# A range guard that tests a bound instead of the last outputs, and a load of its flag that moves ahead of the last eviction

## The chip, the cores and the metric

The kernel runs on one core of one Trainium2 chip. The metric is device time in microseconds for one launch, lower is better. A core has five engines that run in parallel, each through its own queue in order: TensorE (PE; its weight loads are listed as PEld), VectorE (DVE), ScalarE (ACT), GpSimd (POOL) and SyncE (SP, which here issues DMA transfers). Queue entries of an engine's sequencer (loads of registers, branches, semaphores, DMA issues) stand in the profile with a "q" behind the engine's name. PE writes into PSUM, which is divided into banks; DVE and ACT read the banks out ("evict" them) into SBUF, and a bank can take a new matmul only after that.

## The reference

Attention over keys that are pooled 4x4 from an image, with one weight matrix for both keys and values, followed by a gated feed-forward block. Four images, 12288 queries each, 768 pooled keys, 128 channels, 1536 hidden features.

```python
kv_pool = kv.reshape(B, H // r, r, W // r, r, C).mean(axis=(2, 4))
k = v = kv_pool.reshape(B, -1, C) @ w_sr
s = (q @ k.transpose(0, 2, 1)) / np.sqrt(C)
a = np.exp(s - s.max(-1, keepdims=True))
a /= a.sum(-1, keepdims=True) + 1e-09
x = (a @ v).reshape(B * S, D)
out = (np.maximum(x @ w_gate, 0.0) * (x @ w_val)) @ w_out
```

The kernel leaves out the subtraction of the row's maximum and carries x without the division by the row sum: since the block is homogeneous of degree two in x (for positive factors), the output is multiplied at the end by the square of the inverse row sum (`square`, `scale`). That holds only while nothing leaves the range of the 16-bit types, so the kernel ends with a guard: a flag is computed, and if it says that something was out of range, a slow general version (`general`) recomputes everything.

## The kernel before, in words

The 49152 queries are worked in 96 tiles of 512 (`NT` = 96, `k` is the tile's number). Every tile goes through five steps: scores (word `s`, PE) and their exponentials (`e`, ACT, with row sums by accumulation); a DMA transpose of the exponentials on SP (`a_turn`); x, the values weighted by them (`x`, six PE matmuls), evicted to 16 bits by `keep_values` (word `kA`); 12 hidden blocks, each a value matmul `v`, its eviction on ACT `y` (line 142), a gate matmul `g`, and the gated product on DVE `h` (line 526); and 12 output matmuls `o` with the eviction of the output.

The order on every engine is written out by hand, as lists of words. In one pass of the main loop (slot `k`) the words work on different tiles: scores of tile k, x of tile k-2, hidden blocks of tile k-3 (`kF`), output of tile k-4 (`kO`). `STEADY` is the list while there are scores (k < 96), `DRAIN` the list of slots 96 and 97, `LAST` that of slot 98, in which there are only the outputs of tile 94 and the hidden blocks of tile 95, in the order `o v y g h` for block 0, 1, 2 and so on. `out_last` then makes the output of tile 95. The parts of `DRAIN` that matter here are:

```python
... v5 v3 h6 g8 y5 g3 v2 o0 kA y3 o1 v11 g5 y2 h8 y11 o2 v7 ...
... g9 v10 y10 o8 v4 h9 g1 o9 o10 y4 g4 h1 o11 g10 h4 h10 oT
```

Matmul results other than the scores go to six PSUM banks. `bank()` hands out the one that has been in the list of free banks longest, and `freed()` puts a bank at the end of that list where its eviction is written, so the word lists fix which matmul waits for which eviction. The scores have two wide buffers of their own (`wides`).

At the end of a slot, word `oT` evicts the output. For tiles up to 92 that is `out_turn`: a 32x32 block transpose on DVE (line 556), the scaling on POOL (line 561), an addition of the outputs' first columns into `seen` (line 562) and DMA stores, which are handed out one at a time behind the `o` words of the next slot on POOL's and SP's queues (line 946). For tile 93 `out_scale` evicts and scales on DVE (line 593) at the end of slot 97, for tile 94 on ACT (line 591) after `LAST`. `out_store` issues the store and adds a column to `seen` on POOL (line 605). Tile 95 is evicted in three parts by `out_last`: two on DVE, the last on ACT.

The guard before has three sources. `sums_checked` (ACT, lines 832 and 835, in slot 97) tests that the row sums lie between two bounds. `seen_checked` (DVE, lines 838 and 839) turns that, and `seen` (which is infinite or not a number if an output of tiles 0 to 94 was) into 16-bit marks. `last_checked` (line 844) does so for the last part's output, counts the marks with a PE matmul (line 848) and reduces them on DVE to one integer (line 849). `values_load` (line 988) loads it into a register of every engine, and `tc.If` branches on it.

The pooled keys of images 1 to 3 are made during the image before (`image_step`), one pair of key blocks every four slots: loads, sums on POOL, in slot 6 after the pair's beginning a block transpose and a write to DRAM on SP (`turn_blocks`, line 360), then four reads of that block into `kvT` (line 825), which wait in SP's queue for that write, in slot 8 the projection on PE (word `P`) and its eviction on DVE (word `pk`, line 346), and in slots 9 and 11 DMA transposes.

Of the kernel before, what the change touches and what calls it, by code (L numbers as in the profile page):

```python
# [9 lines left out]
FP32 = mybir.dt.float32  # L10
FP16 = mybir.dt.float16
AF = mybir.ActivationFunctionType
ALU = mybir.AluOpType
# [3 lines left out]
def kernel(  # L17
# [23 lines left out]
    nc = tc.nc  # L41

    B, N, C = q.shape
# [15 lines left out]
    LEAD = GRP  # L59
    AT_BUFS = 4  # L60
    qk_scale = 1.0 / math.sqrt(C)
    SUM_MOST, SUM_LEAST = 32.0 * J, J / 8.0

    assert C == 128 and N % T == 0 and J == 128 * NJC and D_FF == 128 * NFB
    assert NFB == 2 * NJC and NST % GRP == 0 and W // r == 8 and HC == 64
# [66 lines left out]
    def freed(ps):  # L132
        free_banks.append(bank_numbers.pop(id(ps))[0])
        return ps
# [310 lines left out]
    def keep_values(k):  # L445
        xT = work.tile([128, NS, 128], FP16, tag="xT", bufs=4, name="xT")
        xTs[k] = xT.rearrange("c s p -> c (s p)")
        nc.vector.tensor_copy(xTs[k], freed(x_banks.pop(k)))  # L448

    x_count = {}  # L450

# [85 lines left out]
    def out_proj(k, fb):  # L537
        if k >= NT - 3:
            if fb == 0:
                o_banks[k] = bank([128, NS, 128])  # L540
            for s in range(NS):
                out_add(k, fb, s, o_banks[k][:, s, :], fb == 0 and s == 0)
            return
        first = k not in o_banks
        if first:
            o_banks[k], o_left[k] = bank([128, T]), NFB
        o_left[k] -= 1
        nc.tensor.matmul(  # L548
            o_banks[k], wo16[:, fb, :], hTs[k][:, fb, :], start=first, stop=o_left[k] == 0
        )  # L550
# [47 lines left out]
    def out_store(k, own, queue=nc.sync):  # L598
        queue.dma_start(
            out[k // GRP * GRP * T : (k // GRP + 1) * GRP * T, :].rearrange(  # L600
                "(p i s) c -> i p s c", p=128, i=GRP
            )[k % GRP][:, own], o_sbs[k][:, own],
        )
        if own.stop == NS and k < NT - 1:
            nc.gpsimd.tensor_tensor(
                seen[:, 0:NS], seen[:, 0:NS], o_sbs[k][:, :, 0], op=ALU.add
            )
        if own.stop == NS:
            for tiles in (hTs, o_banks, o_sbs):
                del tiles[k]  # L610

    def out_last(k):
        parts = [bank([128, 2, 128]), bank([128, 1, 128]), bank([128, 1, 128])]
        owns = [slice(0, 2), slice(2, 3), slice(3, 4)]
        o_banks[k] = None

        def add(s, fb0, fb1):
            n = max(s - 1, 0)
            for fb in range(fb0, fb1):
# [12 lines left out]
        keep(0, nc.vector)  # L632
        add(2, held, NFB)
        keep(1, nc.vector)
        seen_checked()
        add(3, 0, NFB)
        o_sb = o_sbs[k]
        keep(2, nc.scalar, nc.scalar)
        last_checked(o_sb)

    ctx.enter_context(tc.manual_schedule())

# [2 lines left out]
    make_identity(nc, ident)  # L645
    ident16 = const.tile([128, 128], FP16)
    nc.gpsimd.tensor_copy(ident16, ident)
    out_of_range = const.tile([1, 1], mybir.dt.int32)
    ones = const.tile([128, 32], FP16)
    nc.gpsimd.memset(ones, 1.0)  # L650
    lead_scale = const.tile([128, LEAD, NS * 4], FP32)
# [2 lines left out]
    nc.gpsimd.memset(too_much, -SUM_MOST)  # L654
    seen = const.tile([128, NS * 4], FP32)
    nc.gpsimd.memset(seen, 0.0)
    bad = const.tile([128, 2], FP32)
    bad16 = const.tile([128, 22], FP16)
    enough = const.tile([128, 1], FP32)
    nc.gpsimd.memset(enough, SUM_LEAST)  # L660
    nc.gpsimd.memset(kv16[:, :, :, 2 * C : 2 * C + 16], 1.0 / X_SCALE)
# [155 lines left out]
    def image_step(b, at, step):  # L817
        for pair in range(NJC // 2):
            since = at - 4 * pair
            if since in (0, 1) and step in (2, 8):  # L820
                kv_load(b, pair, [2 * since + step // 8])
            elif since in (3, 4) and step == 3:
                pool_pixels(nc.gpsimd, b, pair, since - 3)
            elif since == 6 and moves and step > 4:
                nc.sync.dma_start(*moves.pop())
            elif since in (9, 11) and step == 1:
                turn_values_dma(b, 2 * pair + since // 11)

    def sums_checked():
        past = work.tile([128, NT * NS], FP32, tag="kv_s3", bufs=2, name="past")  # L830
        sums = row_sums.rearrange("t k s -> t (k s)")
        nc.scalar.activation(
            past, sums, AF.Relu, scale=1.0, bias=too_much, accum_out=bad[:, 0:1]
        )
        nc.scalar.activation(past, sums, AF.Relu, scale=-1.0, bias=enough, accum_out=bad[:, 1:2])

    def seen_checked():
        nc.vector.tensor_scalar(bad16[:, 0:2], bad, 0.0, None, op0=ALU.is_gt)
        nc.vector.tensor_scalar(
            bad16[:, 2:18], seen, 0.0, 0.0, op0=ALU.mult, op1=ALU.not_equal  # L840
        )

    def last_checked(o_sb):
        nc.vector.tensor_scalar(
            bad16[:, 18:22], o_sb[:, :, 0], 0.0, 0.0, op0=ALU.mult, op1=ALU.not_equal
        )
        count = wides[0].tile([128, 1024], FP32, tag="wide", name="count_ps")
        nc.tensor.matmul(count[0:1, 0:22], ones[:, 0:1], bad16, start=True, stop=True)
        nc.vector.tensor_reduce(
            out_of_range, count[0:1, 0:22], axis=mybir.AxisListType.X, op=ALU.max  # L850
        )

    def general():
# [74 lines left out]
    for k in range(LEAD + 2, last + 1):  # L928
        g, ph = divmod(k, GRP)
        if ph % 2:  # L930
            q_turn_two(g + 1, ph - 1)
        if ph:
            q_load(g + 2, [[0], [2], [3]][ph - 1])
        b = k // NST + 1
        at = k % NST - 4
        kO, kF, kV = k - LAG - 1, k - LAG, k - 2
        words = STEADY if k < NT else DRAIN if k < last else LAST
        for word in words:
            head, n = word.rstrip("0123456789"), int(word.lstrip("abcdefghijklmnopqrstuvwxyzADPT") or 0)
            if head == "o":  # L940
                out_proj(kO, n)
                if ph == 1 and n == NFB // 2:
                    q_load(g + 2, [1])
                for queue in (nc.gpsimd, nc.sync):
                    if out_moves and n >= 2:
                        queue.dma_start(*out_moves.pop())  # L946
                if spread:
                    spread_scales(*spread.pop(0))
                if b < B:
                    image_step(b, at, n)  # L950
            elif head == "oT":
                if k == last - 1:
                    sums_checked()
                if kO < NT - 3:
                    out_moves.extend(out_turn(kO))
                elif k < last:
                    out_scale(kO, nc.vector, slice(0, NS))
                    out_store(kO, slice(0, NS))
            elif head in ("v", "y", "g", "h"):
                if kF < NT:  # L960
                    {"v": value_proj, "y": keep_value, "g": gate_proj, "h": gated}[head](kF, n)
            elif head in ("s", "e"):
                if k < NT:
                    {"s": score_block, "e": exp_block}[head](k, n)
                    if head == "e" and n % 2:
                        a_turn(k, n - 1, n + 1)
            elif head == "r":
                if LEAD < k <= NT and k % 2 == 0:
                    invert(k - 2)
                    spread += [(k - 2, j) for j in range(4)]  # L970
            elif head in ("tb", "P", "pk"):
                pair, since = divmod(at - 6 if head == "tb" else at - 8, 4)
                if b < B and 0 <= pair < NJC // 2 and since == 0:
                    if head == "tb":
                        moves.extend(turn_blocks(b, pair))
                    elif head == "P":
                        project(b, pair)
                    else:
                        keep_projected(b, pair)
            elif LEAD <= kV < NT:  # L980
                if head == "x":
                    values(kV, n)
                else:
                    keep_values(kV)
    out_scale(last - LAG - 1, nc.scalar, slice(0, NS))
    out_store(last - LAG - 1, slice(0, NS))
    out_last(last - LAG)
    flag = nc.values_load(
        out_of_range[0:1, 0:1],
        skip_runtime_bounds_check_because="it is a count of partitions that is only compared with 0",  # L990
    )
    with tc.If(flag > 0, preferred_fallthrough_block=False):
        general()


# [28 lines left out]
```

## Time and profile before

| what | value |
|---|---|
| time, median of 3 runs | 1026.57 us (1026.33 to 1027.56) |
| time of the profiled execution | 1027.61 us |
| its span on the core | 1025.7 us |
| PE busy | 1017.4 us, 99% |
| ACT busy | 919.4 us, 90% |
| DVE busy | 867.9 us, 85% |
| POOL busy | 545.0 us, 53% |
| granted TensorE clock | 0.998 |
| last 5.7 us (from 1020.0): PE busy in the first 4 us of it | 1.15 us |

The span is what the profile shows between the first and the last recorded instruction; the time of the same execution is 1.9 us longer. Times in the views are us from the span's start. A line of the timeline has start, length, engine, line of the kernel, operation, output and inputs, shape, the number of instructions merged in it and, in brackets, how long the engine was idle before and who ended that. A line of the groups has the busy time of all its instructions, the mean length of one in ns, and the idle time just before them. The chain of waits follows the end of the span back to what released each step; PE makes up 98% of it.

### The profile page before, as it was taken

The numbers are of one execution on the slowest core, as the hardware profiler recorded it, in microseconds if no ns is written. First come the engines' busy times: TensorE is split into PE (matmuls) and PEld (weight loads), VectorE is DVE, ScalarE is ACT, GpSimd is POOL, SyncE is SP. The second block draws the span as 40 slices with busy tenths as digits, with TensorE's granted clock in tenths as the row PEclk, the third lists the DMA queues.
The fourth block names the chain that finished last, engine by engine and source line by source line (L and its number), as shares of the span: only waits on it lengthen the run. The fifth ranks groups of instructions, "written<-read, shape, count | busy, mean of one in ns | idle before, by whom it ended". The sixth has DMA issues, their size and how long they took to land.

```text
span 1025.7 us, 17625 instructions
## 1 busy us (share of the span) xinstructions
PE 1017.4 (99%) x5029; PEld 487.4 (48%) x5029; DVE 867.9 (85%) x1451; ACT 919.4 (90%) x1930; POOL 545.0 (53%) x1410
## 2 busy tenths in 40 slices
PE   8999999999999999999999999999999999999998
PEld 5444444444444444444444444444444444444445
DVE  4888888888888888888888888888888888888897
ACT  4999898989999999999999999989999999999986
POOL 3388857344447576545434856754434543443342
PEclk9999999999999999999999999999999999999999
DMA  9999999987898999788879899977776978776641
GB/s 315 160 176 180 167 207 163 147 127 125 139 194 157 187 180 172 137 127 139 125 132 202 175 176 197 150 134 134 127 132 113 144 118 129 124 128 114 108 83 43
DMA packets 475750, 153.53 MB, mean 150 GB/s; under 512 B 451585, under 2 KB 465921, under 8 KB 475649
## 3 DMA queue, kind: packets, MB, share of 16 engines
q1 hardware_dynamic: 453184, 126.08, 67.6%
q0 software_dynamic: 22032, 25.19, 17.0%
q10 hardware_dynamic: 432, 1.11, 0.3%
q8 instruction: 40, 0.66, 0.3%
q14 instruction: 62, 0.50, 0.2%
HBM read 53.94 MB, written 26.35 MB: 78 GB/s over the span
## 4 chain that ended last, share of the span: by engine, by line
PE 98%; DMA 1%; DVE 0%; issue 0%; SPq 0%; ACT 0%; POOL 0%; DVEq 0%; POOLq 0%
PE bank_ps L507 24%; PE bank_ps L518 24%; PE bank_ps L548 23%; PE wide_ps L398 12%; PE bank_ps L440 12%; DMA kv_in<-in_kv_dram 1%; PE bank_ps L532 1%; PE bank_ps L379 1%; PE bank_ps L457 1%; PE wide_ps L337 0%; PE bank_ps L301 0%; PE bank_ps L315 0%; PE bank_ps L210 0%; PE bank_ps L475 0%; DVE kv_s L273 0%
## 5 line engine op out<-in xcount | busy, mean ns | idle before, releaser
L526 DVE SCALAR_TENSOR_TENSOR hT<-bank_ps,val 128x512 f16<-128x512 f32 x1152 | 728.1, 680 | 104.5 <-PE bank_ps L518 83.9
L142 ACT CAST val<-bank_ps 128x512 f16<-128x512 f32 x1149 | 628.4, 596 | 43.5 <-PE bank_ps L507 23.1
L507 PE MATMUL bank_ps<-xT,wv 128*128 128x512 f16 x1152 | 420.6, 379 | 0.0
L518 PE MATMUL bank_ps<-xT,wg 128*128 128x512 f16 x1152 | 376.0, 379 | 0.0
L548 PE MATMUL bank_ps<-hT,wo 128*128 128x512 f16 x1116 | 348.5, 379 | 0.0
L403 ACT ACTIVATE a<-wide_ps 128x768 f16<-128x768 f32 x368 | 302.1, 821 | 44.1 <-PE wide_ps L398 44.1
L398 PE MATMUL wide_ps<-kv,qT 128*128 128x512 f16 x736 | 179.7, 326 | 0.0
L440 PE MATMUL bank_ps<-aT,kv 128*128 128x512 f16 x552 | 178.8, 379 | 0.0
L548 PEld LDWEIGHTS <-wo 128*128 128x128 f16 x1116 | 109.2, 98 | 132.2 <-issue 1.1
L518 PEld LDWEIGHTS <-wg 128*128 128x128 f16 x1152 | 112.7, 98 | 122.6 <-issue 0.6
L561 POOL TENSOR_TENSOR o_sb<-o_t,scale 128x512 f32<-128x512 f32 x89 | 93.2, 1047 | 140.2 <-issue 122.4
L507 PEld LDWEIGHTS <-wv 128*128 128x128 f16 x1152 | 112.6, 98 | 105.3 <-issue 0.6
L424 POOL COPY scale<-square 32x8 f32<-32x8 f32 x736 | 141.3, 192 | 28.6
L417 POOL TENSOR_TENSOR square<-inverse 128x8 f32<-128x8 f32 x46 | 9.3, 202 | 240.0 <-DVE inverse L415 233.5
L946 POOL DMA_DIRECT2D out_dram<-o_sb x208 | 130.3, 632 | 1.9 <-DMA q<-in_q_dram 1.6
L398 PEld LDWEIGHTS <-qT 128*128 128x128 f16 x736 | 72.0, 98 | 86.9 <-issue 0.2
L448 DVE CAST xT<-bank_ps 128x512 f16<-128x512 f32 x92 | 63.6, 691 | 31.6 <-PE bank_ps L440 31.6
L440 PEld LDWEIGHTS <-kv 128*128 128x128 f16 x552 | 54.0, 98 | 65.1
L403 ACT ACTIVATION_READ_ACCUMULATOR a<-wide_ps 128x1 f32 x368 | 76.1, 207 | 0.0
L556 DVE STREAM_TRANSPOSE o_t<-bank_ps 128x512 f32<-128x512 f32 x93 | 65.4, 703 | 0.2 <-PE bank_ps L507 0.2
L163 POOL DMA_DIRECT2D q<-in_q_dram x84 | 48.8, 581 | 7.1 <-issue 7.1
L257 POOL TENSOR_TENSOR s<-kv_in 128x512 f32<-128x512 f32 x36 | 45.1, 1282 | 0.7
(97 smaller groups left out, 232.9 us busy)
## 6 DMA issues: line engine op xcount, KB each, us to landing
kv_in<-in_kv_dram SPq DMA_DIRECT2D x42, 512.0 KB, 5.3
out_dram<-o_sb SPq DMA_DIRECT2D x177, 64.0 KB, 3.5
q<-in_q_dram POOLq DMA_DIRECT2D x88, 128.0 KB, 4.5
out_dram<-o_sb POOLq DMA_DIRECT2D x176, 64.0 KB, 4.1
aT<-a SPq DMA_TRANSPOSE x184, 5.0
kv_line<-in_kv_dram SPq DMA_DIRECT2D x4, 512.0 KB, 9.9
placed<-blocks SPq DMA_DIRECT2D x9, 128.0 KB, 2.4
kvT<-placed SPq DMA_DIRECT2D x36, 32.0 KB, 1.9
```

The costliest lines, as they stand in the source:

```text
L142: nc.scalar.copy(to, what)
L398: nc.tensor.matmul(s_ps[:, j0 * 128 : j1 * 128], qT, kv16[:, b, j0:j1, 0:C], start=True, stop=True)
L403: nc.scalar.activation(a16s[k][:, s, :], s_banks.pop(s)[:, 0:J], AF.Exp, scale=qk_scale, accum_out=a_sums[k // 2][:, k % 2, s : s + 1],)
L424: nc.gpsimd.tensor_copy(to[32 * b : 32 * (b + 1), :, :, j], squares[k // 2][32 * j : 32 * (j + 1)])
L440: nc.tensor.matmul(x_banks[k], kv16[:, k // NST, jc, C : 2 * C], aT[:, jc], start=first, stop=x_left[k] == 0,)
L507: nc.tensor.matmul(proj_banks["v", k, fb], wv16[:, fb * 128 : (fb + 1) * 128], xTs[k], start=True, stop=True,)
L518: nc.tensor.matmul(proj_banks["g", k, fb], wg16[:, fb * 128 : (fb + 1) * 128], xTs[k], start=True, stop=True,)
L526: nc.vector.scalar_tensor_tensor(hTs[k][:, fb, :], freed(proj_banks.pop(("g", k, fb))), 0.0, vals.pop((k, fb)), op0=ALU.max, op1=ALU.mult,)
L548: nc.tensor.matmul(o_banks[k], wo16[:, fb, :], hTs[k][:, fb, :], start=first, stop=o_left[k] == 0)
L556: nc.vector.transpose(o_t, freed(o_banks.pop(k)))
L561: nc.gpsimd.tensor_tensor(to, o_by, scale.to_broadcast([128, NS, 4, 32]), op=ALU.mult)
L946: queue.dma_start(*out_moves.pop())
```

## The change

- `keep_values` evicts x of tiles 94 and 95 on ACT instead of DVE.
- The outputs of tiles 94 and 95 are no longer looked at (`seen` ends with tile 93). Instead the guard bounds the gated products of these two tiles: per channel the largest |x| of them (`most_of`, one DVE reduction of 128x512 for each tile, at word `oT` of slots 96 and 97; a DVE maximum of the two), times, per block of 256 hidden features, the largest weight of that channel (`widest_of`, twelve DVE reductions of 128x256 over the 16-bit gate and value weights, at word `pk` of slots 74 to 85), summed over the channels by a matmul. The product of the largest sum for the gate and the largest for the value must be at most 60000.
- The test of `seen` (times zero, on POOL) and the row sums' marks go through another matmul. Both matmuls (fp32) stand in PE's queue behind `o6` of `LAST`, and four one-partition DVE steps behind `h5` make one integer, which is now 1 for "in range".
- The flag is loaded inside `out_last`, after the last matmul and ahead of the last eviction on ACT. The branch stays at the end.
- The four reads into `kvT` are issued in slot 7 (from `o2` on) instead of slot 6 (from `o5` on).

```diff
+    SUM_MOST, SUM_LEAST, GATED_MOST = 32.0 * J, J / 8.0, 60000.0
...
     def keep_values(k):
...
-        nc.vector.tensor_copy(xTs[k], freed(x_banks.pop(k)))
+        if k < NT - 2:
+            nc.vector.tensor_copy(xTs[k], freed(x_banks.pop(k)))
+        else:
+            nc.scalar.copy(xTs[k], freed(x_banks.pop(k)))
...
-        if own.stop == NS and k < NT - 1:
+        if own.stop == NS and k < NT - 2:
             nc.gpsimd.tensor_tensor(
                 seen[:, 0:NS], seen[:, 0:NS], o_sbs[k][:, :, 0], op=ALU.add
...
         keep(1, nc.vector)
-        seen_checked()
         add(3, 0, NFB)
-        o_sb = o_sbs[k]
+        flag = nc.values_load(
+            in_range[0:1, 0:1],
...
+        )
         keep(2, nc.scalar, nc.scalar)
-        last_checked(o_sb)
+        return flag
...
+    bad = const.tile([128, 18], FP32)
+    ones32 = const.tile([128, 1], FP32)
+    nc.gpsimd.memset(ones32, 1.0)
...
-            elif since == 6 and moves and step > 4:
+            elif since == 7 and moves and step > 1:
                 nc.sync.dma_start(*moves.pop())
...
+    def widest_of(n):
+        nc.vector.tensor_reduce(
+            widest[:, n : n + 1], (wg16, wv16)[n // NJC][:, n % NJC * 256 : (n % NJC + 1) * 256],
+            axis=mybir.AxisListType.X, op=ALU.max, apply_absolute_value=True,
+        )
+
+    def most_of(k):
+        if NT - 2 <= k < NT:
+            nc.vector.tensor_reduce(
+                most[:, k - NT + 2 : k - NT + 3], xTs[k],
+                axis=mybir.AxisListType.X, op=ALU.max, apply_absolute_value=True,
+            )
+
     def seen_checked():
-        nc.vector.tensor_scalar(bad16[:, 0:2], bad, 0.0, None, op0=ALU.is_gt)
...
+        nc.vector.tensor_tensor(most[:, 0:1], most[:, 0:1], most[:, 1:2], op=ALU.max)
+        nc.gpsimd.tensor_scalar(bad[:, 2:18], seen, 0.0, None, op0=ALU.mult)
+
+    def checked():
+        count = wides[0].tile([128, 1024], FP32, tag="wide", name="count_ps")
+        nc.tensor.matmul(count[0:1, 0:18], ones32, bad, start=True, stop=True)
+        nc.tensor.matmul(
+            count[0:1, 512 : 512 + 2 * NJC], most[:, 0:1], widest, start=True, stop=True
+        )
+        reach = const.tile([1, 2], FP32)
+        nc.vector.tensor_reduce(
+            reach, count[0:1, 512 : 512 + 2 * NJC].rearrange("o (w n) -> o w n", w=2),
+            axis=mybir.AxisListType.X, op=ALU.max,
+        )
+        nc.vector.tensor_reduce(
+            found[:, 0:1], count[0:1, 0:18], axis=mybir.AxisListType.X, op=ALU.add
+        )
         nc.vector.tensor_scalar(
...
+            found[:, 1:2], reach[:, 0:1], reach[:, 1:2], GATED_MOST, op0=ALU.mult, op1=ALU.is_le
+        )
+        nc.vector.scalar_tensor_tensor(
+            in_range, found[:, 0:1], 0.0, found[:, 1:2], op0=ALU.is_le, op1=ALU.mult
         )
...
                 out_proj(kO, n)
+                if k == last and n == 2:
+                    seen_checked()
+                if k == last and n == 6:
+                    checked()
...
                     sums_checked()
+                if NT <= k < last:
+                    most_of(k - 2)
...
                 pair, since = divmod(at - 6 if head == "tb" else at - 8, 4)
+                if head == "pk" and k < NT and 0 <= k - (B - 1) * NST - 2 < 2 * NJC:
+                    widest_of(k - (B - 1) * NST - 2)
...
-    out_last(last - LAG)
-    flag = nc.values_load(
...
-    with tc.If(flag > 0, preferred_fallthrough_block=False):
+    flag = out_last(last - LAG)
+    with tc.If(flag < 1, preferred_fallthrough_block=False):
         general()
```

More of the change, by code (lines that the diff above doesn't have):

```diff
@@ L61 @@
     qk_scale = 1.0 / math.sqrt(C)
-    SUM_MOST, SUM_LEAST = 32.0 * J, J / 8.0
+    SUM_MOST, SUM_LEAST, GATED_MOST = 32.0 * J, J / 8.0, 60000.0
     assert C == 128 and N % T == 0 and J == 128 * NJC and D_FF == 128 * NFB
@@ L634, in out_last @@
         keep(1, nc.vector)
-        seen_checked()
         add(3, 0, NFB)
-        o_sb = o_sbs[k]
+        flag = nc.values_load(
+            in_range[0:1, 0:1],
+            skip_runtime_bounds_check_because="it is 0 or 1 and only compared with 0",
+        )
         keep(2, nc.scalar, nc.scalar)
-        last_checked(o_sb)
+        return flag
     ctx.enter_context(tc.manual_schedule())
@@ L647 @@
     nc.gpsimd.tensor_copy(ident16, ident)
-    out_of_range = const.tile([1, 1], mybir.dt.int32)
+    in_range = const.tile([1, 1], mybir.dt.int32)
     ones = const.tile([128, 32], FP16)
@@ L656 @@
     nc.gpsimd.memset(seen, 0.0)
-    bad = const.tile([128, 2], FP32)
-    bad16 = const.tile([128, 22], FP16)
+    bad = const.tile([128, 18], FP32)
+    ones32 = const.tile([128, 1], FP32)
+    nc.gpsimd.memset(ones32, 1.0)
+    widest = const.tile([128, 2 * NJC], FP32)
+    most = const.tile([128, 2], FP32)
+    found = const.tile([1, 2], FP32)
     enough = const.tile([128, 1], FP32)
@@ L835, in sums_checked @@
         nc.scalar.activation(past, sums, AF.Relu, scale=-1.0, bias=enough, accum_out=bad[:, 1:2])
-    def seen_checked():
-        nc.vector.tensor_scalar(bad16[:, 0:2], bad, 0.0, None, op0=ALU.is_gt)
+    def widest_of(n):
[9 more added lines that the diff above has]
+            )
+    def seen_checked():
+        nc.vector.tensor_tensor(most[:, 0:1], most[:, 0:1], most[:, 1:2], op=ALU.max)
[14 more added lines that the diff above has]
+        )
         nc.vector.tensor_scalar(
-            bad16[:, 2:18], seen, 0.0, 0.0, op0=ALU.mult, op1=ALU.not_equal
+            found[:, 1:2], reach[:, 0:1], reach[:, 1:2], GATED_MOST, op0=ALU.mult, op1=ALU.is_le
         )
[L843 to L850, printed above, removed]
+        nc.vector.scalar_tensor_tensor(
+            in_range, found[:, 0:1], 0.0, found[:, 1:2], op0=ALU.is_le, op1=ALU.mult
         )
@@ L986 @@
     out_store(last - LAG - 1, slice(0, NS))
-    out_last(last - LAG)
[L988 to L991, printed above, removed]
-    with tc.If(flag > 0, preferred_fallthrough_block=False):
+    flag = out_last(last - LAG)
+    with tc.If(flag < 1, preferred_fallthrough_block=False):
         general()
```

## The prediction

> **What bounds the kernel now.** First the page's busy table and its costliest groups.
>
> ```profile
> PE 1017.4 (99%) x5029; PEld 487.4 (48%) x5029; DVE 867.9 (85%) x1451; ACT 919.4 (90%) x1930; POOL 545.0 (53%) x1410
> ...
> L507 PE MATMUL bank_ps<-xT,wv 128*128 128x512 f16 x1152 | 420.6, 379 | 0.0
> ```
>
> TensorE (PE) has work from end to end: its 1152 value matmuls have 0.0 us idle ahead of them. Two kinds of change move the end: what makes PE late, and what follows its last matmul (a stretch that I call the tail). So next the timeline of the last 5 us, the lines of the flag's load and of the program's end.
>
> ```profile
> 1020.29 0.62 DVE L593 TENSOR_TENSOR o_sb<-bank_ps,square 128x256 f32<-128x256 f32 x2 [0.90 <-PE bank_ps L532]
> ...
> 1021.07 0.37 ACT L591 ACTIVATE o_sb<-bank_ps,square 128x128 f32<-128x128 f32 x1 [1.31 <-POOL seen L605]
> 1021.17 0.38 SPq L599 DMA_DIRECT2D out_dram<-o_sb  x1
> 1021.47 0.36 ACTq L599 DMA_DIRECT2D out_dram<-o_sb  x1
> 1021.47 0.17 DVE L844 TENSOR_SCALAR bad<-o_sb 128x4 f16<-128x4 f32 x1 [0.40 <-ACT o_sb L591]
> 1021.69 0.17 PE L848 MATMUL count_ps<-bad,ones 128*1 128x22 f16 x1 [0.71 <-DVE bad L844]
> 1021.90 0.17 DVE L849 TENSOR_REDUCE out_of_range<-count_ps 1x1 int32<-1x22 f32 x1 [0.26 <-PE count_ps L848]
> ...
> L988 SPq TENSOR_LOAD <-out_of_range x1: 482/482/482, 1022.1 to 1022.1; - x1
> ...
> L1019 SPq EVENT_SEMAPHORE  x12: 27/28/28, 1023.5 to 1024.2; - x12
> L1019 SPq DRAIN  x2: 7/10/13, 1024.3 to 1024.3; - x2
> ...
> L1019 POOLq DRAIN  x1: 1692/1692/1692, 1023.2 to 1023.2; - x1
> ```
>
> The last matmul ends at 1020.98. After it comes a chain: the eviction, three guard steps, the flag's load on every engine at 1022.1, a branch, and the end. GpSimd's (POOL's) drain of 1.69 us starts at 1023.2 and ends at 1024.9; SyncE (SP) is through with its semaphores at 1024.35 and waits 0.6 us for that. 0.8 us of closing semaphores bring the span to 1025.74. The last store (1021.47) lands by 1023.2, the row's 1.7 us.
>
> Last the places where VectorE (DVE) and ScalarE (ACT) feed PE after the last attention tile.
>
> ```profile
> 994.13 1.07 ACT L142 CAST val<-bank_ps 128x512 f16<-128x512 f32 x2 [0.90 <-PE bank_ps L507]
> ...
> 995.44 0.38 PE L518 MATMUL bank_ps<-xT,wg 128*128 128x512 f16 x1
> ...
> 1009.82 1.29 DVE L526 SCALAR_TENSOR_TENSOR hT<-bank_ps,val 128x512 f16<-128x512 f32 x2
> 1011.03 0.68 DVE L593 TENSOR_TENSOR o_sb<-bank_ps,square 128x512 f32<-128x512 f32 x1
> 1011.62 1.28 DVE L526 SCALAR_TENSOR_TENSOR hT<-bank_ps,val 128x512 f16<-128x512 f32 x2
> ...
> 1011.76 0.10 PEld L507 LDWEIGHTS <-wv 128*128 128x128 f16 x1 [0.17 <-DVE o_sb L593]
> ```
>
> A 512-wide DVE step starts 0.60 us after the one before (1011.03, 1011.62), a cast on ACT 0.48 us after (1.07 for two less 0.59 for one). At 1011.76 PE stands waiting for DVE's L593: there DVE's lateness is PE's at once.
>
> **The change, part by part.**
>
> Tail. Flag and guard leave it. POOL can load the flag, branch and drain (1.69 us) while PE still works on the last tile. What is left is SP: its last store is issued at 1021.17 for 0.38 us, then it loads the flag at 1021.60 instead of 1022.10, and its whole walk moves by 0.50 us: done at 1023.86, with the store landed by 1023.2. The closing 0.8 us then start 1.06 us earlier than now (1024.95 less 1023.86, less 0.03 for the signal). Term: -1.06. ACT's load goes ahead of the last eviction: 0.49 us between 1019.76, where the eviction before ends, and 1021.07; hidden, and without the cover it would be up to 0.5. Bounds: -1.1, and 0 if POOL's drain is tied to the others' end.
>
> The x casts of tiles 94 and 95 move from DVE (L448) to ACT, in word kA of DRAIN, behind y5 and ahead of y3. They put y3 and what follows 0.48 us back. The six banks go out in the order in which they came free; walking DRAIN's words, g5 takes the bank that y3 frees. y3 (the second cast of 994.13) ends at 995.20, g5 starts at 995.44: a reserve of some 0.2. PE is 0.28 late, and 0.05 more at v7, behind y2. Term +0.33. In the second drain tile (g5 at 1004.52, y3 over at 1004.27) the same gives +0.32. Bounds: 0 (the cast slips into one of ACT's gaps, 0.87 to 0.90 us just ahead of y5) and +0.48 each.
>
> DVE gets 0.60 back per cast, and gives it for `most_of`, a reduction of 128x512, at oT. In tile 96 it delays L556's transpose by 0.6, but the next user of that bank has a reserve of 0.4 and DVE catches up where its cast was: in the +0.32. In tile 97 it stands between h10 (1010.43) and L593 (1011.03), where PE waits already, and the relief came 7 us too early (DVE follows its inputs after 1005, so it was not ahead). Term +0.60. No row shows such a reduction; bounds: 0.2, the start-to-start of L849 on 22 elements, and 1.2, two casts; I take the cast, which has as many elements. The Trainium skill, "VectorE: DVE Perf Modes", section "The perf-mode tier table", says that a reduction has no faster mode for 16-bit data, only one element a cycle, which speaks against placing it here. By it the price is the cast's, with a mode of two elements a cycle it would be near 0.33 and the sum 0.27 less; no row here shows which.
>
> Guard in the last tile. Two fp32 matmuls in PE's queue after o6, at most 0.1 us each by L301's 0.11 us steps; their inputs are ready (DVE's maximum behind h1, POOL's product after L605 at 1012.06, ACT's sums since 1010.9). DVE then gets four one-partition steps between h5 and h6: two free ones at 0.07 us (L838 to L839), two that need the result before them at some 0.2 (0.17 and a signal), 0.54 in all. DVE's reserve per step is 0.05 (12 steps in 7.77 us against 0.60 each), and PE's v9 takes the bank of h6 (over at 1016.12) at 1016.36: 0.19. So 0.54 - 0.05 - 0.19 = +0.30 on PE, the matmuls' 0.2 inside it, for what waits on PE isn't late twice. Bounds +0.1 and +0.7. The 30 matmuls of `out_last` before h10 leave 0.4 us for DVE to be level again.
>
> `widest_of`: twelve reductions 128x256, one in each of tiles 74 to 85, at word pk. L346, a DVE step of that width at that word, took 0.34 us start to start (168.76 to 169.11), and PE stood still after one of nine. But those tiles hold an extra projection, which gives DVE time that here is missing; the walk leaves about 0.30 of reserve at pk, so 0.00 to 0.05 each. Term +0.3 (0 to +0.6).
>
> Image. Four kvT reads in nine places leave the tile in which SP waits for the block's write.
>
> ```profile
> SPq L825 <- DMA placed<-blocks: 20.3, 9, 3.7
> ```
>
> That frees 2.3 us of SP each time, past two transposes of a and one of q, whose users come a tile or more later. PE shows no wait on any of it, and the projection still has a tile's length after the reads. Term 0 (-0.5, the few stalls in the middle of the trace, to +0.2). A memset on POOL in the opening, 0.1 us, is hidden: POOL waits there for DVE until about 10 us.
>
> Sum: -1.06 + 0.33 + 0.32 + 0.60 + 0.30 + 0.3 = +0.8 us. The span of 1025.7 becomes 1026.5. The profiled run took 1027.61, which is 1.04 over the median of the three runs; +0.8 on that median is 1027.4. The terms on PE are lateness that small gaps may take up, so I go a little lower: 1027.2.
>
> **Rivals.**
>
> All is hidden but the tail: the banks' reserves hold the added work. 1026.57 - 1.06 = 1025.5. For it: ACT's gaps, DVE's 15% of idle time. Against: those gaps stand elsewhere, and PE already waits for L593.
>
> Nothing comes off the tail: POOL's 1.69 us drain ends when the other engines do, wherever it starts. 1026.57 + 1.85 = 1028.4. For it: no other engine's drain is over 0.09 us. Against: nothing that POOL started is open then.
>
> Slower: reductions cost more than a cast of the same size. It is `widest_of` that decides: above the 0.30 of reserve each 0.1 us makes PE 1.2 us later over twelve tiles. With 0.45 us for 256 elements the sum is 0.8 + 12 x 0.105 = +2.06, and from there on the kernel is slower than a measurement's noise. At two cycles an element (0.6 and 1.1 us) it is 0.8 + 3.2 + 0.9 = +4.9, or 1031.5. For it: no row of a long reduction. Against: cast, gate product and transpose all take one element a ns.
>
> The flag says out of range, and everything is computed again: milliseconds. The bound (a sum over channels of the largest |x| by the widest weight) lies far under 60000 for weights and inputs of this size.
>
> **How the numbers follow.** Forecast 0.70 (1026.5 to 1028.3 by the bounds), all hidden 0.14, nothing off the tail 0.08, dear reductions 0.06, the rest 0.02. The range takes in the rival below and most of the one above: 1025.6 to 1028.6. 0.2% is 2.05 us, about what a measurement of this kernel can tell from no change. All but the dear reductions and the far ends of the others stay inside: same 0.86, slower 0.10, faster 0.04 (a gain from the image's move that I can't see).
>
> **What would show it.** Right: POOL's drain over before PE's last matmul, SP's twelve semaphores ending the span, PE idle ahead of L518 near 995.5 and 1004.8 for about 0.3 us each, 0.6 us more ahead of the third value matmul of the last tile, 0.3 us after the counts; each 128x512 reduction near 0.60 us. Wrong: PE's last matmul at its old distance from the start, a drain of POOL still at the end, or the twelve tiles with `widest_of` more than 0.06 us longer than the tiles after them.

## Result, and the profile after

| what | before | after |
|---|---|---|
| time, median of 11 runs each, alternating | 1026.40 us (1026.22 to 1027.56) | 1029.06 us (1028.19 to 1030.34) |
| time of the profiled execution | 1027.61 us | 1029.25 us |
| its span | 1025.7 us | 1027.5 us |

The ratio is 1.0025, 95% interval 1.0016 to 1.0035: the change makes the kernel 2.7 us slower. The prediction was 1027.2 (1025.6 to 1028.6), so it gave too low a time.

Two measures are used from here on, both read from the trace. The **PE part** is the time from the first value matmul of the 61st hidden tile, in the steady middle of the run, to the end of PE's last output matmul: 372.39 us before, 374.33 after, **+1.94**. The **tail** is the time from that end to the end of the span: 4.76 us before, 5.58 after, **+0.82**. Together +2.76, which is the difference of the medians (+2.66). The spans differ by 1.8 only, since the profiled execution of before lost about 1.0 us more in its opening than most others.

The PE part first. Busy table and groups of the page of after:

```profile
PE 1017.8 (99%) x5032; PEld 486.7 (47%) x5032; DVE 870.5 (85%) x1464; ACT 921.3 (90%) x1932; POOL 545.1 (53%) x1411
...
L510 PE MATMUL bank_ps<-xT,wv 128*128 128x512 f16 x1152 | 420.8, 379 | 0.7 <-DVE o_sb L596 0.6
```

PE's work is the same but for three count matmuls in the records. What was 0.0 us of idle time before the value matmuls is 0.7, and 0.6 of it is one wait for an eviction on DVE (L596, the L593 of before). The timeline of after shows that wait, what stands ahead of it on DVE, and the other places where PE is late (start, length, engine, line):

```profile
994.60 0.38 PE L510 MATMUL bank_ps<-xT,wv 128*128 128x512 f16 x1
995.09 0.38 PE L521 MATMUL bank_ps<-xT,wg 128*128 128x512 f16 x1
...
1001.58 0.68 DVE L854 TENSOR_REDUCE most<-xT 128x1 f32<-128x512 f16 x1
1002.17 0.71 DVE L559 STREAM_TRANSPOSE o_t<-bank_ps 128x512 f32<-128x512 f32 x1
...
1011.07 0.68 DVE L854 TENSOR_REDUCE most<-xT 128x1 f32<-128x512 f16 x1
1011.66 0.68 DVE L596 TENSOR_TENSOR o_sb<-bank_ps,square 128x512 f32<-128x512 f32 x1
...
1012.39 0.39 PE L510 MATMUL bank_ps<-xT,wv 128*128 128x512 f16 x1 [0.60 <-DVE o_sb L596]
```

Value to gate matmul is 0.22 us start to start where nothing is late; 994.60 to 995.09 is 0.49, that is 0.27 late: the x cast on ACT. The two reductions take 0.59 us start to start (1001.58 to 1002.17, 1011.07 to 1011.66), and the second one puts L596 and with it PE's matmul at 1012.39 back by as much.

Now the tail. The timeline of after, its last lines:

```profile
1021.21 0.62 DVE L596 TENSOR_TENSOR o_sb<-bank_ps,square 128x256 f32<-128x256 f32 x2 [0.89 <-PE bank_ps L535]
1021.98 0.37 ACT L594 ACTIVATE o_sb<-bank_ps,square 128x128 f32<-128x128 f32 x1 [1.31 <-PEq L1027]
1022.38 0.36 ACTq L602 DMA_DIRECT2D out_dram<-o_sb  x1
```

PE's last matmul ends at 1021.89, and the last store is issued 0.49 us behind it, as before (1021.47 behind 1020.98). The guard's steps are gone from here. Next the line of the program's end (L1054) by queue: number of instructions, shortest, median and longest in ns, first and last start.

```profile
L1054 POOLq DRAIN  x1: 1687/1687/1687, 1017.7 to 1017.7; - x1
...
L1054 SPq EVENT_SEMAPHORE  x8: 28/28/28, 1024.0 to 1024.4; - x8
L1054 SPq EVENT_SEMAPHORE  x4: 27/28/28, 1026.2 to 1026.5; - x4
L1054 SPq DRAIN  x2: 7/10/13, 1026.6 to 1026.7; - x2
```

POOL's drain is over 2.5 us before PE ends, as meant. But SP's twelve semaphores, 0.7 us in one piece before, fall into eight and four with 1.8 us between. What they wait for is in the DMA issues of after (KB, us from issue to landing); the same store took 1.7 us before:

```profile
out_dram<-o_sb ACTq DMA_DIRECT2D x1, 64.0 KB, 4.0
```

A store is shared out over 16 DMA engines, and the trace has a completion for each share. Of SP's last store 15 shares are there 1.90 us behind PE's end, the 16th at 4.32; of ACT's, 2.42 and 4.49. The DMA queues of after show what went first: packets and queues (packets, MB, share of 16 engines) in the stretch from 1023.72 to 1025.03, and then in that from 1025.03 to 1026.40 (SP's stores are on q1, ACT's on q10).

```profile
DMA packets 4, 0.04 MB, mean 31 GB/s; under 512 B 0, under 2 KB 0, under 8 KB 0
## 3 DMA queue, kind: packets, MB, share of 16 engines
q14 instruction: 3, 0.02, 8.3%
q8 instruction: 1, 0.02, 5.4%
...
DMA packets 18, 0.01 MB, mean 6 GB/s; under 512 B 2, under 2 KB 18, under 8 KB 18
## 3 DMA queue, kind: packets, MB, share of 16 engines
q1 hardware_dynamic: 9, 0.00, 2.6%
q10 hardware_dynamic: 9, 0.00, 1.6%
```

In the first stretch only instruction code is fetched (8 KB packets on q14, 16 KB on q8) and not one packet of a store starts, though 18 are left, nine for one share of each of the last two stores. In the second these 18 go, and no code. The hold begins ahead of the code packets, though: SP's last store has no packet that starts between 1.44 and 3.14 us behind PE's end, where before the change the last of them starts at 1.45, and the first code packet is on record only at 1.83. What holds the share in between, the trace doesn't show.

The fetches follow the engines' jump to the program's end (the last branch of each engine, timed by its end): DVE and PE now jump 0.53 us behind PE's last matmul, ACT 1.09, SP 1.60, and code packets start at 1.83, 2.02, 2.11 and 2.88. Before, all five engines jumped between 1.81 and 2.35, and the packets started at 2.92 to 3.11, when the last store had landed (2.19).

### The profile page after: what moved, and what is told of

It reads as the page before. It is cut to its first block, busy times and chain, and to the rows that moved or that the text cites. A ratio compares the mean times of both kernels' runs of the same rounds, so it can differ in the third digit from the quotient of the medians.

```text
span 1027.5 us, 17650 instructions
## 1 busy us (share of the span) xinstructions
PE 1017.8 (99%) x5032; PEld 486.7 (47%) x5032; DVE 870.5 (85%) x1464; ACT 921.3 (90%) x1932; POOL 545.1 (53%) x1411
```

## The experiments

All are given as the time less that of the kernel before from the same batch (1026.18 to 1026.40), with the PE part and the tail of the profiled execution.

| run | less before, us | ratio and interval | PE part | tail |
|---|---|---|---|---|
| after | +2.66 | 1.0025 (1.0016 to 1.0035) | 374.33 | 5.58 |
| tail only | +0.90 | 1.0007 (0.9998 to 1.0016) | 372.63 | 5.40 |
| tail only, late jump | -0.66 | 0.9995 (0.9986 to 1.0004) | 372.63 | 3.71 |
| after, late jump | +0.83 | 1.0009 (1.0000 to 1.0018) | 374.33 | 3.71 |
| image move alone | -0.04 | 1.0001 (0.9992 to 1.0010) | 372.38 | 4.76 |
| POOL late too | +1.97 | 1.0017 (1.0007 to 1.0026) | 374.33 | 4.88 |
| x back on DVE | +0.48 | 1.0005 (0.9996 to 1.0014) | 373.87 | 3.73 |
| reductions moved | -0.27 | 0.9997 (0.9987 to 1.0006) | 373.24 | 3.70 |
| all steps moved | -0.48 | 0.9995 (0.9986 to 1.0004) | 373.07 | 3.71 |
| only ACT late | +2.62 | 1.0022 (1.0012 to 1.0032) | 374.32 | 5.42 |
| ACT and DVE late | +2.47 | 1.0025 (1.0013 to 1.0037) | 374.32 | 3.97 |
| ACT and PE late | +0.99 | 1.0012 (1.0002 to 1.0022) | 374.34 | 3.71 |
| maximum later | -0.36 | 0.9995 (0.9986 to 1.0004) | 373.01 | 3.71 |

### Tail only

The kernel before with the early flag alone: no bound on tiles 94 and 95, x on DVE, no reductions, image as before. Its guard covers the row sums and the outputs of tiles 0 to 93 only. Against the changed kernel:

```diff
-        if k < NT - 2:
-            nc.vector.tensor_copy(xTs[k], freed(x_banks.pop(k)))
-        else:
-            nc.scalar.copy(xTs[k], freed(x_banks.pop(k)))
+        nc.vector.tensor_copy(xTs[k], freed(x_banks.pop(k)))
...
-                if NT <= k < last:
-                    most_of(k - 2)
...
-                if head == "pk" and k < NT and 0 <= k - (B - 1) * NST - 2 < 2 * NJC:
-                    widest_of(k - (B - 1) * NST - 2)
```

> The kernel before with the early flag alone: the guard covers the row sums and the outputs of tiles 0 to 93, nothing looks at tiles 94 and 95; x stays on DVE, no reductions, kvT reads in slot 6 as before; flag computed behind o6 of the last tile and loaded ahead of the last eviction. PE should be at most 0.15 us late (one count matmul). Theory F (an engine's early jump to the program's end brings its instruction fetch forward, and the fetches hold one DMA engine just when the last two stores need it): the last store still lands some 4 us after its issue, the tail after PE's last matmul is some 5.5 us as in the changed kernel, time about 1027.2 (+0.8). The tail term of the prediction as it stood (-1.06): about 1025.4.

1027.12 us. Its end line and its last store:

```profile
L1033 SPq EVENT_SEMAPHORE  x8: 27/28/28, 1022.0 to 1022.4; - x8
L1033 SPq EVENT_SEMAPHORE  x4: 28/28/28, 1024.1 to 1024.4; - x4
...
out_dram<-o_sb ACTq DMA_DIRECT2D x1, 64.0 KB, 3.8
```

The same gap and the same late landing without anything else of the change: the early flag, meant to shorten the tail, lengthens it by 0.64 us. The time alone would not show it (the interval of the ratio holds 1). The PE part is 0.24 longer, where at most 0.15 was expected, and it is one step: between the value matmuls around the two passes of the fp32 count matmul PE takes 0.88 us instead of 0.66.

### Tail only, late jump

The same, but ACT loads the flag behind its last store, and DVE and PE get small steps that depend on the last eviction ahead of their loads; POOL and SP stay as they are. They are there to delay the jumps; the PE part stays what it was (372.63).

```diff
+        o_sb = o_sbs[k]
+        keep(2, nc.scalar, nc.scalar)
+        nc.vector.tensor_copy(late[:, 0:1], o_sb[:, 3, 0:1])
+        for n in range(3):
+            nc.vector.tensor_copy(late[:, n + 1 : n + 2], late[:, n : n + 1])
+        count = wides[0].tile([128, 1024], FP32, tag="wide", name="held_ps")
+        nc.tensor.matmul(count[0:1, 0:1], ones32, late[:, 3:4], start=True, stop=True)
         flag = nc.values_load(
...
-        keep(2, nc.scalar, nc.scalar)
```

> As e1, but ACT loads the flag after its last store, and DVE (four tiny copies in a row that begin with the last evicted part) and PE (one matmul that reads the last copy) end only after the last eviction; POOL still loads, branches and drains early. Theory F: the jumps of PE, DVE and ACT come about a us later, their fetches after the stores, the last store lands 1.7 us after its issue, the tail is some 3.7 us, time about 1025.4. If the stores are slow for another reason (POOL's early end, the order of the queues), landing stays near 4 us and the time equals that of e1 or is above it.

1025.56 us. Its end line and last store:

```profile
L1040 SPq EVENT_SEMAPHORE  x12: 27/28/28, 1021.9 to 1022.6; - x12
...
out_dram<-o_sb ACTq DMA_DIRECT2D x1, 64.0 KB, 1.7
```

More instructions, and 1.56 us less. The jumps of ACT, DVE and PE are now at 1.66, 1.93 and 2.48 behind PE's end, the code packets at 2.63 to 3.20, behind the landing (2.19), and the tail is 3.71: the predicted -1.06, measured as -1.05, exists once the jumps no longer bring code ahead of the store.

### After, late jump

The changed kernel with those same steps.

> The changed kernel with the hold of e2. Theory F: its tail falls from 5.6 to some 3.7 us while PE stays 1.9 us late, so about 1027.2, 1.8 under the changed kernel. If the tail isn't about the fetches: 1029.

1027.05 us. SP's twelve semaphores run from 1023.6 to 1024.3 in one piece, the tail is 3.71 again, and the PE part is that of the changed kernel to the hundredth. So 1.9 of its 2.7 us are the collision at the end (5.58 less 3.71; by the medians 2.0), and the rest is the PE part less the gain in the tail (1.94 - 1.05 = +0.89, measured +0.83).

### Image move alone

The kernel before with the four reads in slot 7.

```diff
-            elif since == 6 and moves and step > 4:
+            elif since == 7 and moves and step > 1:
```

> The kernel before with the kvT reads in slot 7 alone. The prediction's term is 0 (-0.5 to +0.2): 1026.4 within 0.3, with no PE idle time in slots 6 to 8. A rival that the image's move costs something: over 1026.9.

1026.18 us against 1026.22: no difference that can be measured, and none in the PE part (372.38).

### POOL late too

The late jump with POOL held as well, by one more copy, so that its drain falls at the end as before the change.

```diff
+        nc.gpsimd.tensor_copy(late[:, 4:5], late[:, 3:4])
         flag = nc.values_load(
```

> e3 with POOL held back too: a tiny copy that reads the last of DVE's four comes ahead of its load of the flag. The prediction has POOL's drain of 1.69 us in the tail of the kernel before. If a late POOL sets the end, it loads near 1.4 us after PE's last matmul, jumps near 2.1, drains to 4.2 and the span ends near 5.0 us after the last matmul, 1.3 over e3: 1028.4. If the drain ends with the other engines wherever it starts (the prediction's second rival), nothing changes against e3: 1027.05.

1028.23 us, 1.2 more than with POOL early. Its end line:

```profile
L1062 SPq EVENT_SEMAPHORE  x12: 27/28/28, 1024.8 to 1025.5; - x12
...
L1062 POOLq DRAIN  x1: 1687/1687/1687, 1025.1 to 1025.1; - x1
```

The drain starts at 1025.1 and ends at 1026.8, with SP through at 1025.6: now POOL sets the end. The tail is 4.88, with the last store landed in time. So the rival in which POOL's drain is tied to the others' end is refuted: moved to the front it takes 1.2 us off, and it was not the cause of the slow tail.

### x back on DVE

The late jump, and x of tiles 94 and 95 evicted by DVE as before.

```diff
-        if k < NT - 2:
-            nc.vector.tensor_copy(xTs[k], freed(x_banks.pop(k)))
-        else:
-            nc.scalar.copy(xTs[k], freed(x_banks.pop(k)))
+        nc.vector.tensor_copy(xTs[k], freed(x_banks.pop(k)))
```

> e3 with x of tiles 94 and 95 evicted on DVE as before, all else as in e3. By the prediction's terms for the two drain tiles (+0.33 and +0.32, of which 0.16 in the second is also DVE's reduction ahead of the transpose), PE ends 0.48 us earlier: 1026.6, and the waits of PE near 994.6 and 1004.2 are gone. If the casts on ACT cost nothing and DVE alone is late, it ends 0 to 0.6 us later, since DVE gets two casts more: 1027.1 to 1027.7.

1026.74 us; the PE part is 0.46 shorter, 0.35 of it in the first drain tile (9.45 to 9.10 between its first value matmul and the next tile's), 0.10 in the second. There 0.24 us stay, and the place is in the timeline of this run:

```profile
1001.88 0.83 PE L507 MATMUL bank_ps<-xT,wv 128*128 128x512 f16 x2
1002.55 0.59 PE L518 MATMUL bank_ps<-xT,wg 128*128 128x512 f16 x2
```

Two value matmuls that take 0.59 elsewhere take 0.83: PE waits for the transpose L556, which stands behind the reduction of tile 94 on DVE. The changed kernel has the same 0.83 at 1002.48.

### Reductions moved

In addition the reductions over x stand behind h0 of slot 96 and h5 of slot 97 instead of at `oT`.

```diff
+        (NT, "h0"): [lambda: most_of(NT - 2)],
+        (NT + 1, "h5"): [lambda: most_of(NT - 1)],
...
-                if NT <= k < last:
-                    most_of(k - 2)
```

> e6 with the two reductions over x moved from the ends of the slots to places where DVE waits for its inputs (behind h0 in slot 96, behind h5 in slot 97). By the term +0.60 (PE waits there for the eviction behind the reduction) and the 0.16 of the drain tile before it, PE ends 0.75 us earlier than in e6: 1025.8; the wait of 0.76 us ahead of the last tile's third value matmul falls to the 0.17 of the kernel before. If a reduction costs its time wherever it stands: 1026.6.

1025.99 us; the PE part is 0.63 shorter. The wait in the second drain tile is gone, and the 0.77 us ahead of the third value matmul of the last tile fall back to the 0.17 that the kernel before has there. A longer wait comes one block earlier: the value matmul at 1009.90 has its successor at 1010.36 instead of 1010.12, 0.24 late, where the kernel before is 0.08 late (1010.87 to 1011.16).

### All steps moved

In addition `widest_of` at word `tb` of the same slots, the maximum of the two reductions behind h9 of slot 97, the counts behind g2 of the last tile, and the small DVE steps one per block.

```diff
-                if head == "pk" and k < NT and 0 <= k - (B - 1) * NST - 2 < 2 * NJC:
+                if head == "tb" and k < NT and 0 <= k - (B - 1) * NST - 2 < 2 * NJC:
...
+        (NT + 1, "h9"): [lambda: most_checked()],
+        (last, "g0"): [lambda: seen_checked()],
+        (last, "g2"): [lambda: reach_counted(), lambda: bad_counted()],
+        (last, "h3"): [lambda: reach_kept()],
```

> e7 with widest_of at word tb instead of pk, the two count matmuls behind g2 of the last tile, and the small DVE steps one at a time behind h9 of slot 97 and h3, h4, h5 and h6 of the last. The whole guard is there. By the reserves of the banks only the two matmuls (0.15 us) stay on PE, and the tail is that of e3 (3.7 us): 1025.3, under both kernels. If small steps cost their time wherever they stand: 1025.8 as e7.

1025.78 us, where 1025.3 was expected. The tiles with `widest_of` take what they took before the change (134.74 us for 13 tiles against 134.75, and 135.08 in the changed kernel), so those 0.33 us are gone. But the last part of PE grew by 0.19 instead of getting shorter (11.22 to 11.41), and the timeline shows PE waiting for a gated product:

```profile
1009.52 0.38 PE L507 MATMUL bank_ps<-xT,wv 128*128 128x512 f16 x1
1010.05 0.38 PE L518 MATMUL bank_ps<-xT,wg 128*128 128x512 f16 x1 [0.15 <-DVE hT L526]
```

### Maximum later

I took that wait for the price of the maximum behind h9, and moved it behind h1 of the last tile, with the counts and small steps one block later.

```diff
-        (NT + 1, "h9"): [lambda: most_checked()],
-        (last, "g2"): [lambda: reach_counted(), lambda: bad_counted()],
+        (last, "h1"): [lambda: most_checked()],
+        (last, "g3"): [lambda: reach_counted(), lambda: bad_counted()],
```

> The kernel with all steps moved, but the maximum of the two reductions is placed behind h1 of the last tile (as in the changed kernel) instead of behind h9 of slot 97, and the counts and small steps follow one block later than there. Theory (that maximum made PE wait 0.32 us ahead of a gate matmul near 1009.5): the last part of PE falls from 11.41 to 11.1 us, PE is 0.3 us earlier, time 1025.5. Rival (the step costs PE the same wherever it stands, since DVE has no idle time left there): 1025.8.

1025.82 us: nothing gained, and the theory fell. Of the 0.31 (0.53 less 0.22) only 0.06 went with the maximum; the same place still has 0.25, as the run with the reductions moved has 0.24 without any such step:

```profile
1009.42 0.38 PE L507 MATMUL bank_ps<-xT,wv 128*128 128x512 f16 x1
1009.89 0.38 PE L518 MATMUL bank_ps<-xT,wg 128*128 128x512 f16 x1
```

By these three runs it comes with the reduction of 128x512 behind h5, which no run removed alone; that it is this reduction is argued, not shown.

### Whose jump it is: ACT late, DVE late, PE late

Three runs of the changed kernel hold only some of the engines. First only ACT: its load stands behind its last store.

```diff
+        o_sb = o_sbs[k]
+        keep(2, nc.scalar, nc.scalar)
         flag = nc.values_load(
...
-        keep(2, nc.scalar, nc.scalar)
```

> The changed kernel, but the flag's load stands behind the last eviction on ACT (as before the change); DVE and PE still load it and jump to the end some 1.4 us earlier than with all engines held. Theory (the fetches that follow an engine's end jump by 1.1 to 1.5 us hold a share of the last two stores back when they reach the DMA engine first): DVE's and PE's fetches still start near 1.8 and 2.0 us behind PE's last matmul, so the last landing stays beyond 3.5 us and the tail between 4.7 and 5.6. Rival (ACT's own early load and jump, ahead of its store's landing, is what delays it): last landing near 2.2, tail 3.7.

1028.80 us, tail 5.42: the last landing is at 4.33, code packets start at 1.65 and 2.00 and last 0.94 and 1.07 us. ACT's early load and jump are not the cause.

Then ACT and DVE (the copies of the late jump, without the matmul), so that only PE jumps early:

> As the run with only ACT late, and DVE is held too; only PE jumps early. Theory: PE's 16 KB fetch near 2.0 us, alone, still holds the shares that have not moved by then: last landing 2.9 to 3.9, tail 4.1 to 5.1. Rival (the DVE fetch that comes first, near 1.8, is the one that does it): last landing 2.2, tail 3.7.

1028.65 us, tail 3.97, and neither theory's case came about: PE's 16 KB packet (told from the others by its size and their times) started already 0.58 us ahead of PE's last matmul, and 0.97 us ahead of PE's own jump at 0.39. Why it came so early isn't shown. There it met the stores ahead of the last two. The DMA issues of this run for the last three stores:

```profile
out_dram<-o_sb SPq DMA_DIRECT2D x1, 128.0 KB, 2.6
out_dram<-o_sb SPq DMA_DIRECT2D x1, 64.0 KB, 2.3
out_dram<-o_sb ACTq DMA_DIRECT2D x1, 64.0 KB, 2.2
```

They take 2.6, 2.3 and 2.2 us to land; in the changed kernel the 128 KB store takes 1.9, and in the late-jump run the last takes 1.7. So these three stores land 0.5 to 0.7 us later, with a single code packet of 1.0 us near them. That the packet costs all of it is argued, not shown: of the last two, the other 15 shares are 0.2 to 0.3 us late as well, and SP took 0.62 us to issue its last store instead of 0.38. The profiled execution also lost 1.2 us in its opening, and the two measures explain only 1.1 of the 2.47 us in the table. The other five executions lie between 1027.95 and 1029.92, and where they lost the rest is not on record.

Last ACT and PE (the matmul, without the copies), so that only DVE jumps early:

> As the run with only ACT late, and PE is held too; only DVE jumps early. Theory: its 8 KB fetch near 1.8 us ends by about 2.6 when it has the DMA engine to itself; last landing 2.4 to 3.2, tail 3.7 to 4.4. Rival (PE's 16 KB fetch alone does it): last landing 2.2, tail 3.7. Both fall if the landing stays beyond 3.5.

1027.17 us, tail 3.71, the last landing at 2.20. The end line of this run, and its DMA queues from 1023.2 to 1024.0:

```profile
L1057 SPq EVENT_SEMAPHORE  x12: 27/28/28, 1023.7 to 1024.4; - x12
...
DMA packets 26, 0.02 MB, mean 21 GB/s; under 512 B 9, under 2 KB 25, under 8 KB 25
## 3 DMA queue, kind: packets, MB, share of 16 engines
q14 instruction: 1, 0.01, 6.0%
q10 hardware_dynamic: 25, 0.01, 4.0%
```

DVE's 8 KB packet starts at 1.63 and takes 0.77 us, and beside it the store's packets go through and land in time. So DVE's early jump alone cost nothing here, as the rival of this run has it, and with ACT held, holding PE as well was enough; whether the packet met a store on the same DMA engine the trace doesn't tell. Whether PE's 16 KB packet does it alone, or only with DVE's ahead of it, no run settles, since the one meant for that had its packet elsewhere. But the packets point at PE's: in the three runs with a late landing the held share goes on just when the 16 KB packet ends (3.14 and 3.15 us behind PE's end in the changed kernel, 2.97 and 2.97 in the tail alone, 3.03 and 3.07 with only ACT late), while DVE's packet has ended by 2.67, 2.58 and 2.59.

## Why the prediction was wrong

**The step that failed is the tail term, -1.06, in its words "done at 1023.86, with the store landed by 1023.2".** It measured +0.82. The working moved the engines' loads and branches and kept the store's landing from the row of before (1.7 us). The landing was not a constant: the earlier jumps bring code packets to the DMA engines while the last two stores are still on their way, one share in 16 is held until the 16 KB packet has passed, and SP's semaphores wait for that share until 1026.2. That the jumps cause the late landing is shown by the runs that hold them; that the packet itself is in the way rests on the times at which it ends and the share goes on. All three runs in which DVE and PE jump early together (the changed kernel, the tail alone, only ACT late) have it, with tails of 5.4 to 5.6. The runs that hold both have 3.7, or 4.9 with POOL held too. The rest of the term was right: POOL's drain is off the path, SP sets the end, and the gain is 1.05 where the store lands in time.

The page "Runtime: NRT & Kernel Launch" of the Trainium skill, section "Instruction fetch mechanics", says that a taken branch whose target is not in the window forces a DMA fetch of the target page. The packets of the kernels before and after the change agree with it: before the change they start 0.7 to 1.2 us behind the jumps, after it 1.0 to 1.5 (the 16 KB packet taken as PE's, the others in order of time). PE's packet does not always follow the jump: with DVE and ACT late it starts 0.97 us ahead of it, with x back on DVE 0.34 us ahead (2.24 and 2.58 behind PE's end).

**The x casts on ACT (+0.33 and +0.32).** The first is right in place and size: 0.27 ahead of g5 and 0.06 at v7. The second tile lost 0.33, close to the 0.32 foreseen, but that is luck: 0.24 comes from `most_of` of tile 94 ahead of the transpose, which the prediction had absorbed in the reserve of the next user's bank, and only 0.10 from the cast. With x back on DVE the first tile is level and the second keeps its 0.24.

**`most_of` ahead of L593 (+0.60).** Right: 0.59 us start to start, and PE's wait ahead of the third value matmul grew from 0.17 to 0.77. The price that the Trainium skill gives in "VectorE: DVE Perf Modes", section "The perf-mode tier table", one element a cycle for a reduction and so the cast's price (0.60), is the one that held; the 0.33 of a faster mode did not.

**The guard in the last tile (+0.30).** The size is right, +0.27, but by luck, since the place is wrong. It is not DVE's four steps that cost: they run from 1016.01 to 1016.51 and PE goes on at 0.66 us per block right behind. The step between the value matmuls around the counts takes 0.93 us instead of 0.66: it is PE's own time for the fp32 count matmuls. The tail alone, with one of the two, has 0.23 there.

**`widest_of` (+0.3).** +0.33, 0.03 for each, by 0.33 us start to start against 0.34 foreseen. **Image (0).** 0.

**The step from the sum to the forecast** ("a little lower", 1027.4 to 1027.2) had the wrong sign in the PE part: it came out at 1.94 against 1.85, so on balance no gap took any of it up. With the measured tail in place of the predicted one the sum gives 1026.4 + 1.85 + 0.82 = 1029.1, and 1029.06 was measured.

**The rivals.** "Nothing comes off the tail" is nearest in time (1028.4), but its mechanism is refuted by the run with POOL late. "All is hidden" and dear reductions are out by the PE part. None of the rivals had the tail itself get longer. (The prediction's "one element a ns" is too fast for its own rows: 512 elements at 0.60 us start to start are 1.2 ns each.)

Every step moved and the jumps held, the same bound costs 0.68 us on PE instead of 1.94 and the kernel is at 1025.78, 0.48 below the kernel before; the ratio 0.9995 (0.9986 to 1.0004) doesn't tell that from no change.

## What to carry to other kernels

An engine that is finished early and leaves the program is not free of effect: its way to the end fetches code through the DMA engines that still carry the last output. When work is taken off a kernel's end, look at which transfers are still open at the time of each engine's last jump, and hold an early engine's jump back so that its code comes behind the store's landing (here a single small matmul on PE, with ACT's load behind its store, was enough). And price the landing of the last store anew: a duration from a row holds for the traffic that stood beside it there.

## What was not expected of the hardware

- One late share of 16 sets a store's landing: 15 shares are there at 1.90 us, the last at 4.32 behind PE's end, after its nine packets had been held until 3.14, when a 16 KB code packet ended (3.15).
- At the program's end an 8 KB code packet took 0.31 to 0.94 us and a 16 KB one 0.96 to 1.36 us.
- Four small copies on DVE and one matmul on PE, added at the very end, with ACT's load behind its store, made the kernel 1.6 to 2.0 us faster (tail only 1027.12 to 1025.56, the changed kernel 1029.06 to 1027.05).
- POOL's drain at the end of the program is 1.69 us whenever it is run, in every trace (1687 to 1693 ns).
- The opening varies by up to 1.5 us between profiled executions (647.1 to 648.6 us from the start to the 61st hidden tile). Its cause was not looked for.
